# Two weight loads on two DMA queues at once, and the activations behind the first of them

## The chip, the cores and the metric

The kernel runs on one core of a Trainium2 chip. The metric is the device time of one execution in microseconds; a comparison is made between medians of runs. A core has five engines that run their own instruction streams and meet at semaphores: TensorE (PE in the profile), VectorE (DVE), ScalarE (ACT), GpSimd (POOL) and SyncE (SP). A transfer between memory and the on-chip buffer is issued by an engine's instruction stream into that engine's DMA queue; here SyncE's queue is q1 and ScalarE's is q10 in the profile's table. The same 16 DMA engines serve both.

## What is computed

One decoding step for a batch of two tokens: attention over a cache of 8192 keys for 32 heads of width 128, multiplied by a gate from a small MLP.

```
xn = layernorm(x)                                  # x: 2 x 512
q  = xn @ wq                                       # 512 x 4096, 32 heads of 128
p  = softmax(q . k_cache * 128**-0.5)              # k_cache: 2 x 32 x 8192 x 128, fp32
s  = (p . v_cache) @ wo                            # v_cache the same size, wo: 4096 x 512
y  = layernorm(xn)
g  = silu(gelu(y @ w1 + b1) @ w2 + b2)             # w1: 512 x 1376, w2: 1376 x 512
out = x + s * g
```

The two caches are 537 MB of the 559 MB that are read.

## The kernel before

The kernel writes out every engine's order by hand. Each operation is put on record with the keys that it reads and writes, and a small planner (`Plan.op`) derives the semaphore waits from these keys; the instructions of each engine are then emitted in the order in which they were recorded. The order of the code is therefore the order on each engine and on each DMA queue.

The caches are worked off in 32 tiles, each of two heads of one token (a "pair" here): a tile of K is 128 partitions by 64 KB, 8.39 MB, and so is a tile of V. There are two K buffers, `kb[0]` and `kb[1]`, and one V buffer, `vb`. For each pair n, VectorE multiplies the K tile by q in place in two halves (L510), sums each product over the head width (L516) and takes the maximum (L520, L525). ScalarE takes the exponentials (L535). TensorE multiplies them with the V tile (L551). K of pair n+2 is issued by SyncE when the sums of pair n are done; V of pair n is issued when L551 of pair n-1 is done. All of these loads pass through the one helper `load` (L315) on SyncE's queue.

Before the first pair there is a start-up in which no V tile is in `vb` yet, and the MLP's weights and rows lie there instead. wq lies in `kb[0]`, the buffer into which K of pair 1 goes. The order of SyncE's queue at the start is w1, w2, wq, K of pair 0 in two halves (into `kb[1]`), then K of pair 1, which waits until the q projection (L480) has read wq, then V of pair 0, which waits for the last reader of the MLP's tiles. ScalarE's queue carries x (4 KB, two rows), b1 and b2.

The compute of the start-up is one chain. x is copied into a second layout (L380, L382); layer norm (L361 to L366) gives xn, a second layer norm gives y; both are transposed on TensorE and copied by ScalarE (L373, L374). Then, on TensorE in this order: the first MLP product with w1 (L408, with b1 at L410), the rearrangement of its result and the GELU, the second product with w2 (L450) and b2 (L460), the q projection (L480), and the spreading of q over all partitions into `Q` (L493, L495). VectorE's first L510 waits for the first part of `Q` and for K of pair 0.

After the last pair, wo is loaded into `vb` in five pieces and the output projection (L621, L630) and the gate close the kernel.

Of the kernel before, what the change touches and what calls it, by code (L numbers as in the profile page):

```python
# [20 lines left out]
class Plan:  # L21
# [18 lines left out]
    def op(self, eng, fn, r=(), w=(), over=(), it=None, dma=None):  # L40

        o = Op()
        o.eng, o.fn, o.it, o.dma, o.tell = eng, fn, it, dma, False
        need = {}

        def after(d, war):
            if d.dma is None and dma is None and d.eng == eng and (eng == "pe" or war):
                return
            if d.dma is None:
                if need.get(d.eng) is None or need[d.eng].idx < d.idx:  # L50
                    need[d.eng] = d
            else:
                k = ("dma", d.dma)
                if need.get(k) is None or need[k].idx < d.idx:
                    need[k] = d

        for k in r:
            if k in self.writer:
                after(self.writer[k], False)
        for k in list(w) + list(over):  # L60
            if k in self.writer:
                after(self.writer[k], False)
            for d in self.readers.get(k, ()):
                after(d, True)
        clock = self.clock[eng]
        need = {k: d for k, d in need.items() if clock.get(k, 0) < d.idx}
        o.deps = [(k, d) for k, d in need.items()
                  if not any(e is not d and e.done.get(k, 0) >= d.idx for e in need.values())]
        for _, d in o.deps:
            for k, v in d.done.items():  # L70
                clock[k] = max(clock.get(k, 0), v)
        own = eng if dma is None else ("dma", dma)
        self.count[own] = o.idx = self.count.get(own, 0) + 1
        o.done = dict(clock)
        o.done[own] = o.idx
        for k in w:
            self.writer[k] = o
            self.readers[k] = []
        for k in r:
            if k not in w:  # L80
                self.readers.setdefault(k, []).append(o)
        self.ops.append(o)
# [87 lines left out]
def decode_kernel(nc, x, kc, vc, wq, wo, w1, b1, w2, b2, out):  # L170
    P = 128
# [27 lines left out]
    plan = Plan(nc)  # L199
    op = plan.op  # L200
# [7 lines left out]
    def act(fn, r=(), w=()):  # L208
        op("act", fn, r, w)
# [53 lines left out]
    def take(name, p, n, base=0, at=None):  # L263

        if at is None:
            at = used[0]
            used[0] += n
            assert used[0] <= KP * DH
        boot.append(name)
        return vb[base:base + p, at:at + n]  # L270

    w1_sb = take("w1", P, ND * F).rearrange("p (c f) -> p c f", f=F)
    w2_sb = take("w2", P, WB * P)
# [3 lines left out]
    x_sb, xn, y = (take(k, B, D, 0, at + D * i) for i, k in enumerate(("x", "xn", "y")))  # L277
# [26 lines left out]
    def bank():  # L304
        i = turn[0] % 4
        turn[0] += 1
        return scratch[i], f"s{i}"
# [3 lines left out]
    vf = vc.rearrange("b h s d -> (b h s d)").rearrange("(n p j d) -> n p j d", p=P, j=KP, d=DH)  # L311
    M = KP // 2

    def load(dst, src, sem, w, over=()):
        op("sp", lambda: nc.sync.dma_start(dst, src), (), w, over=over, dma=sem)  # L315

    def load_k(n, halves=False):
        i = (n + 1) % 2
        if halves:
            for s in range(2):  # L320
                load(kbuf[i][:, s * M:(s + 1) * M], kf[n][:, s * M:(s + 1) * M], f"k{i}{s}", [("kb", i, s)])
        else:
            load(kbuf[i], kf[n], f"k{i}", [("kb", i, s) for s in range(2)])
# [4 lines left out]


    load(w1_sb, w1.rearrange("(p c) f -> p c f", p=P), "w1", ["w1"])  # L330
    load(w2_sb, w2.rearrange("f n -> (f n)").rearrange("(p e) -> p e", p=P), "w2", ["w2"])
    load(wq_sb, wq.rearrange("(p c) n -> p c n", p=P), "wq", [("kb", 0, s) for s in range(2)])
    load_k(0, halves=True)


    dve(lambda: nc.vector.memset(eps_t, EPS), w=["eps"])
    act(lambda: nc.scalar.activation(warm, eps_t, AF.Sqrt), ["eps"], ["warm"])
    op("act", lambda: nc.scalar.dma_start(x_sb, x.rearrange("b s d -> (b s) d")), w=["x"], dma="x")
    for t, src, k in ((b1_sb, b1, "b1"), (b2_sb, b2, "b2")):
        op("act", lambda t=t, src=src: nc.scalar.dma_start(  # L340
            t.rearrange("o (k e) -> o k e", k=16), src.rearrange("(o k e) -> o k e", o=1, k=16)), w=[k], dma=k)
# [144 lines left out]
    for k in range(N // NB):  # L486

        b, e = divmod(k, HH // NB)
        i, g = divmod(e, GQ)
        p, kp = bank()  # L490
# [114 lines left out]
    for b in range(B):  # L605
# [7 lines left out]
                                        op=ALU.mult), ["OA", "rl"], ["on"])  # L613
# [27 lines left out]
    for b in range(B):  # L641
        eng = "sp" if b % 2 == 0 else "act"
# [29 lines left out]
```

## Time and profile before

| what | value |
|---|---|
| time, median of 3 runs | 1300.59 us (1300.42 to 1301.28) |
| profiled execution, its own time | 1301.38 us |
| its span | 1299.3 us |
| DVE busy | 1132.8 us, 87% of the span |
| PE busy | 404.6 us, 31% |
| ACT busy | 77.7 us, 6% |
| DMA | 559.39 MB, mean 431 GB/s |

The span is the stretch between the first and the last instruction that the profiler recorded; the execution's own time has 2.1 us more around it. Shares of busy time are averages over the start-up, 32 pairs and the end. A row of the chain of waits tells what the program was waiting for at each time, followed back from the last instruction; a row of the timeline has the start in us, the duration, the engine, the line, the operation with its tiles, and in brackets how long the engine had been idle and what released it. In the table of DMA issues a landing is the time from the issue to the semaphore that tells that all data are there.

### The profile page before, as it was taken

The numbers are of one execution on the slowest core, as the hardware profiler recorded it, in microseconds if no ns is written. First come the engines' busy times: TensorE is split into PE (matmuls) and PEld (weight loads), VectorE is DVE, ScalarE is ACT, GpSimd is POOL, SyncE is SP. The second block draws the span as 40 slices with busy tenths as digits, with TensorE's granted clock in tenths as the row PEclk, the third lists the DMA queues.
The fourth block names the chain that finished last, engine by engine and source line by source line (L and its number), as shares of the span: only waits on it lengthen the run. The fifth ranks groups of instructions, "written<-read, shape, count | busy, mean of one in ns | idle before, by whom it ended". The sixth has DMA issues, their size and how long they took to land.

```text
span 1299.3 us, 6271 instructions
## 1 busy us (share of the span) xinstructions
PE 404.6 (31%) x2708; PEld 121.7 (9%) x2708; DVE 1132.8 (87%) x273; ACT 77.7 (6%) x250; POOL 1.4 (0%) x8
## 2 busy tenths in 40 slices
PE   5602333312333311333321333321333331233336
PEld 1100001000101000101000101100001100010102
DVE  3599989988889988889988888988888988888990
ACT  1100000000000000000000000000000000000000
POOL 0000000000000000000000000000000000000000
PEclk9856666556666556666655666655666655666658
DMA  9999999999999999999999999999999999999998
GB/s 408 443 422 444 428 438 430 428 444 424 444 428 436 432 428 444 424 444 428 436 432 428 442 426 444 426 438 430 430 440 428 442 428 438 430 430 440 424 434 346
DMA packets 10831, 559.39 MB, mean 431 GB/s; under 512 B 1212, under 2 KB 1220, under 8 KB 1480
## 3 DMA queue, kind: packets, MB, share of 16 engines
q1 hardware_dynamic: 10808, 559.29, 99.6%
q8 instruction: 3, 0.05, 0.0%
q14 instruction: 4, 0.03, 0.0%
q10 hardware_dynamic: 16, 0.01, 0.0%
HBM read 559.30 MB, written 0.00 MB: 430 GB/s over the span
## 4 chain that ended last, share of the span: by engine, by line
DMA 74%; PE 24%; issue 0%; DVE 0%; ACT 0%; SPq 0%
DMA vb<-in_A_v_cache_dram 72%; PE po L551 22%; DMA vb<-in_A_wo_dram 2%; PE s L408 1%; DMA vb<-in_B_w_dram 1%; PE po L480 1%; PE s L450 0%; PE wide L621 0%; PE s L410 0%; DVE vb L416 0%; PE acc L630 0%; ACT L429 0%; PE s L457 0%; DVE vb L442 0%; PE s L422 0%
## 5 line engine op out<-in xcount | busy, mean ns | idle before, releaser
L510 DVE TENSOR_TENSOR kb<-kb,Q 128x8192 f32<-128x8192 f32 x64 | 555.5, 8681 | 107.1 <-DMA kb<-in_A_k_cache_dram 98.9
L516 DVE TENSOR_REDUCE sc<-kb 128x64 f32<-128x8192 f32 x64 | 552.3, 8666 | 0.0
L551 PE MATMUL po<-vb,PZ 128*8 128x512 f32 x1984 | 282.9, 734 | 301.4 <-DMA vb<-in_A_v_cache_dram 301.4
L530 PE MATMUL s<-nm,srow 1*128 1x2 f32 x64 | 18.6, 358 | 364.7 <-DVE nm L525 364.7
L551 PEld LDWEIGHTS po<-vb,PZ 128*8 128x8 f32 x1984 | 56.6, 103 | 501.6 <-issue 501.6
L522 PE MATMUL s<-ident,mx 128*1 128x128 f32 x32 | 11.9, 372 | 182.0 <-DVE mx L520 182.0
L556 ACT COPY o<-po 128x512 f32<-128x512 f32 x32 | 18.7, 585 | 546.8 <-PE po L551 546.8
L530 PEld LDWEIGHTS s<-nm,srow 1*128 1x128 f32 x64 | 15.9, 306 | 374.1 <-DVE nm L525 374.1
L531 ACT COPY bias<-s 128x2 f32<-128x2 f32 x32 | 5.1, 160 | 612.1 <-PE s L530 612.1
L558 PE MATMUL s<-mod,o 128*128 128x2 f32 x256 | 33.7, 254 | 22.8 <-ACT o L556 22.8
L558 PEld LDWEIGHTS s<-mod,o 128*128 128x128 f32 x256 | 31.0, 191 | 52.5 <-ACT o L556 52.5
L535 ACT ACTIVATE PZ<-sc,bias 64x128 f32<-64x128 f32 x64 | 25.5, 399 | 1.8
L522 PEld LDWEIGHTS s<-ident,mx 128*1 128x1 f32 x32 | 2.5, 79 | 185.5 <-DVE mx L520 155.0
L565 DVE TENSOR_TENSOR Z<-blk,s 128x8 f32<-128x8 f32 x32 | 4.9, 152 | 12.8 <-PE s L558 12.8
L416 DVE COPY vb<-vb 2x384 f32<-2x384 f32 x4 | 1.8, 500 | 16.1 <-ACT vb L412 16.1
L408 PE MATMUL s<-vb 128*2 128x512 f32 (+1 forms) x24 | 12.4, 669 | 0.6 <-DMA vb<-in_B_w_dram 0.6
L535 ACT ACTIVATION_READ_ACCUMULATOR PZ<-sc,bias 64x1 f32 x64 | 11.8, 185 | 0.0
L639 DVE TENSOR_TENSOR gate<-acc,gate 128x128 f32<-128x128 f32 x1 | 0.3, 292 | 12.9 <-PE acc L630 12.9
L520 DVE TENSOR_REDUCE mx<-sc 128x1 f32<-128x128 f32 x32 | 9.1, 286 | 1.1
L539 ACT ACTIVATE ZR<-half,rs 128x8 f32<-128x8 f32 x32 | 9.6, 300 | 1.0
L551 PE MATMUL po<-kb,PZ 128*8 128x512 f32 x64 | 9.0, 726 | 1.4 <-ACT PZ L535 1.4
L621 PE MATMUL wide<-vb,on 128*2 128x512 f32 x52 | 7.9, 719 | 3.9 <-DMA vb<-in_A_wo_dram 3.9
(83 smaller groups left out, 79.8 us busy)
## 6 DMA issues: line engine op xcount, KB each, us to landing
kb<-in_A_k_cache_dram SPq DMA_DIRECT2D x4, 4096.0 KB, 43.6
kb<-in_A_v_cache_dram SPq DMA_DIRECT2D x2, 4096.0 KB, 41.2
vb<-in_B_w_dram SPq DMA_DIRECT2D x2, 2752.0 KB, 12.5
vb<-in_A_wo_dram SPq DMA_DIRECT2D x1, 4096.0 KB, 19.5
vb<-in_A_wo_dram SPq DMA_DIRECT2D x1, 2560.0 KB, 25.3
vb<-in_A_wo_dram SPq DMA_DIRECT2D x1, 1024.0 KB, 27.3
vb<-in_A_wo_dram SPq DMA_DIRECT2D x2, 256.0 KB, 27.5
vb<-in_A_v_cache_dram SPq DMA_DIRECT2D x31, 29.5
```

Of the source, the lines that this page charges most:

```text
L408: pe(lambda f=f, w=w, ph=ph, c=c: matmul(ph[:B, :w], yT[:, c, :], w1_sb[:, c, f:f + w], start=(c == 0), stop=False), ["yT", "w1"], [k])
L480: pe(lambda i=i, c=c, wv=wv, a=a, j=j, hd=hd: matmul(PO[R * j:R * j + NQ * B, :].rearrange("m (h d) -> m h d", d=DH), xnT[:, c, a:a + NQ * ...
L510: dve(lambda: nc.vector.tensor_tensor(out=k, in0=k, in1=Q[:, n].unsqueeze(1).to_broadcast([P, M, DH]), op=ALU.mult), [("kb", i, s), ("Q", ...
L516: dve(lambda: nc.vector.tensor_reduce(out=SC[n % 2][:, s * M:(s + 1) * M], in_=k, axis=AX.X, op=ALU.add), [("kb", i, s)], [("sc", n % 2, s)])
L520: dve(lambda: nc.vector.tensor_reduce(out=MX, in_=SC[n % 2], axis=AX.X, op=ALU.max), [("sc", n % 2, 0), ("sc", n % 2, 1)], ["mx"])
L522: pe(lambda: transpose(PM[:1, :P], MX, ident), ["mx", "ident"], ["s1"], it)
L530: pe(lambda: matmul(PN[:, :U], srow, NM, start=True, stop=True), ["srow", "nm"], ["s2"], it)
L535: act(lambda r=r, s=s: nc.scalar.activation(PZ[r, :, s, :], sc[r], AF.Exp, bias=BIAS[r, s:s + 1], scale=SCALE, accum_out=RS[r]), ["bias", ...
L539: act(lambda: nc.scalar.activation(ZR[b][:, UP * hp:UP * (hp + 1)], half, AF.Copy, scale=RS), ["half"] + [("rs", s) for s in range(U)], [( ...
L551: pe(lambda t=t, j=j, v=v: matmul(PO[R * j:R * j + U * JW, :], PZ[:, t].rearrange("p s j -> p (s j)"), v[:, t * JW:(t + 1) * JW, :].rearra ...
L556: act(lambda: nc.scalar.copy(O4, PO), ["po"], ["o4"])
L558: pe(lambda i=i: matmul(PT[:, :U], O4[:, i * DH:(i + 1) * DH], mod[:, i:U * JW:JW], start=(i == 0), stop=(i == JW - 1)), ["o4", "mod"], [" ...
```

## The change

w2's load is issued by ScalarE, as the first instruction of its stream, while SyncE issues w1. x's load moves from ScalarE, where it stood behind the warm-up activation, to SyncE, between w1 and wq. b1 and b2 stay on ScalarE's queue and stand behind w2 there. `load` takes the issuing engine as an argument. No computing instruction is added, removed or reordered; below the edit, all line numbers are one higher.

```diff
-    def load(dst, src, sem, w, over=()):
-        op("sp", lambda: nc.sync.dma_start(dst, src), (), w, over=over, dma=sem)
+    def load(dst, src, sem, w, over=(), eng="sp"):
+        op(eng, lambda: plan.eng[eng].dma_start(dst, src), (), w, over=over, dma=sem)
...
     load(w1_sb, w1.rearrange("(p c) f -> p c f", p=P), "w1", ["w1"])
-    load(w2_sb, w2.rearrange("f n -> (f n)").rearrange("(p e) -> p e", p=P), "w2", ["w2"])
+
+    load(w2_sb, w2.rearrange("f n -> (f n)").rearrange("(p e) -> p e", p=P), "w2", ["w2"], eng="act")
+    load(x_sb, x.rearrange("b s d -> (b s) d"), "x", ["x"])
     load(wq_sb, wq.rearrange("(p c) n -> p c n", p=P), "wq", [("kb", 0, s) for s in range(2)])
     load_k(0, halves=True)
...
     act(lambda: nc.scalar.activation(warm, eps_t, AF.Sqrt), ["eps"], ["warm"])
-    op("act", lambda: nc.scalar.dma_start(x_sb, x.rearrange("b s d -> (b s) d")), w=["x"], dma="x")
```

## The prediction

> **What bounds the kernel now.** I read the strip of forty slices first, then the queue table, then the chain of waits in order of time, and last the timeline and the waits of the first 60 us, where every edited line runs.
>
> From the page, the strips and the queue table:
> ```profile
> DMA  9999999999999999999999999999999999999998
> GB/s 408 443 422 444 428 438 430 428 444 424 444 428 436 432 428 444 424 444 428 436 432 428 442 426 444 426 438 430 430 440 428 442 428 438 430 430 440 424 434 346
> ...
> q1 hardware_dynamic: 10808, 559.29, 99.6%
> ```
> The 16 DMA engines are busy from the first slice to the last but one, on SyncE's queue alone (q1). So 559 MB at 431 GB/s is the time. Work on another engine is free until it makes the queue run dry; then each microsecond of dry queue is a microsecond at the end, because a queue that is always full cannot make up for it.
>
> The chain of waits, in order of time (start us, us, what):
> ```profile
> 0.73 9.48 DMA vb<-in_B_w_dram
> 10.27 6.24 PE s L408 x8
> ...
> 17.45 3.52 PE s L408 x8
> ...
> 38.75 7.02 PE po L480 x64
> 45.79 0.33 SPq L315
> 46.16 48.96 DMA vb<-in_A_v_cache_dram
> 95.12 0.12 issue
> 95.24 9.92 PE po L551 x64
> 105.18 28.65 DMA vb<-in_A_v_cache_dram
> 133.83 0.12 issue
> 133.95 9.34 PE po L551 x64
> 143.31 29.23 DMA vb<-in_A_v_cache_dram
> ```
> w1 opens the MLP at 10.27; the MLP and then the q projection (L480) end at 45.79; only then may K of head pair 1 be issued, into wq's buffer, and V0 behind it. V0 lands at 95.12, V1 at 133.83: 38.71 us for one K and one V tile, so 19.35 us a tile.
>
> The waits of SyncE's own queue say the same from its side:
> ```profile
> SPq L315 <- PE po L480: 42.4, 1, 42.4
> ```
> SyncE has issued w1, w2, wq and K0 in the first 3 us and then stands 42.4 us for L480. These 22.4 MB are the cover for all of the start. Its end: 95.12 less two tiles of 19.35 is 56.4; the longest landing among the first K issues, 53.5 us after an issue at about 2.6, gives 56.1. I take **56.2 for the landing of K0's second half**.
>
> The timeline of the first 12 us (start, us, engine, line, operation), first the x chain:
> ```profile
> 0.89 0.56 ACTq L338 DMA_DIRECT2D vb<-in_A_x_dram  x1
> 4.61 0.60 PE L380 MATMUL s<-vb,ident 2*2 2x128 f32 x8 [4.61 <-DMA vb<-in_A_x_dram]
> 9.66 0.17 ACT L374 COPY vb<-s 128x8 f32<-128x8 f32 x1 [1.44 <-PE s L373]
> 10.27 6.24 PE L408 MATMUL s<-vb 128*2 128x512 f32 x8 [0.64 <-DMA vb<-in_B_w_dram]
> ```
> x lands at 4.61 and is layer-normed twice and transposed by 9.83, which with one handover (0.07) is 9.90: 5.3 us after x. That hides inside w1's own transfer with 0.37 us to spare. The answer for the tile vb in the first 20 us has the landings of w1 and w2:
> ```profile
> DMA to landing us min/median/max: 9.5/12.5/15.6
> ```
> w1 takes 9.5, w2 15.6 from an issue at 1.2, so 16.8 on the clock: 6.6 us for w2's 2.82 MB behind w1. With eight rows on each of 16 DMA engines, a row is 0.82 us. The rest of w1's 9.48, that is 2.9 us, is fixed: issue to first byte, and last byte to release.
>
> **The change, part by part.**
>
> *w2 from SyncE to ScalarE.* SyncE saves an issue (0.4 us), ScalarE gains one ahead of its table load and warm-up activation, which nothing waits for; both 0 on the path. w2 is needed first by L450 at 31.6, 15 us after it lands, so an earlier w2 is worth nothing. Bytes are the same, so w1 and w2 together are done at 16.8 as before, but w1 now shares. If rows alternate, w1's eighth row is the 15th of 16, and w1 lands at 16.0 instead of 10.2. b1 and b2, issued behind w2 on ScalarE's queue, land near 17; L410 wants b1 only after eight L408 matmuls. 0.
>
> *x from ScalarE to SyncE, behind w1.* The costly part. x is two rows of 2 KB on one ring each, where w1's rows stand ahead of it. It lands with or just after w1: between 16.0 and 16.9 by sharing, I take 16.6. Lower bound 10.3, if w1 keeps the whole rate; upper bound 17.7, one more row. So x is 12.0 us later, and its 5.3 us of layer norm and transposes, which used to lie under w1, now stand behind both weights: L408 starts at 16.6 + 5.3 = 21.9 instead of 10.27, **11.6 later**.
>
> *From L408 to the issue of K1.* 45.79 - 10.27 = 35.5 us of PE, ACT and DVE work, unchanged. wq still lands at about 36.2, by its 34.5 us from 1.65, and L480 starts after that in both kernels. One term floats: matmuls after an idle stretch are slow at first. L408's first eight take 6.24 and the next eight 3.52, a surcharge of 2.7; L551's 64, which also start after idleness, take 8.40 to 9.92 in the chain. So a cold start may be up to 1.5 us cheaper or dearer, and L408's is near the dear end. There is a second cold start at L450. I take -0.3, bounds -1.6 and +1.2. **K1 is issued 11.3 later, at 57.1.**
>
> [...]
>
> *What is late next.* K1 cannot land before its issue plus 2.9 plus 19.35: 57.1 + 2.9 = 60.0, where the queue ran dry for landings at 56.2. **Gap: 60.0 - 56.2 = 3.8 us** (bounds with x at 10.3: none, as 51.1 + 2.9 is 54.0; with x at 17.7 and a dear clock: 6.4). It opens once L480 ends more than 7.5 us late.
>
> *Whether a second gap follows.* DVE starts head pair 0 when Q is there, 11.3 later. K2's issue moves from 82.8 to 94.1; with 2.9 it is 97.0, before V0 lands at 95.1 + 3.8 = 98.9: covered by 1.9. The maximum for pair 0 (DVE, 91.57) moves to 102.9, its exponentials follow 2.2 later, so L551 starts at 105.1, no longer when V0 lands, and ends 9.9 later at 115.0. V1 then needs 117.9; K2 keeps the queue until 98.9 + 19.35 = 118.3. Covered by only 0.4. K3 (117.65 becomes 129) is covered by 6. DVE needs 35 us a pair (82.76 to 117.65) against the DMA's 38.7, so it regains 3.7 each time and its 7.5 us of lag behind the DMA are gone after two pairs. No second gap, and nothing of the first is won back, since the DMA then runs full to the end.
>
> **Sum.** The profiled execution took 1301.38 (span 1299.3 and 2.1 around it). Plus 3.8 is 1305.2. The median of the three runs shown is 0.8 lower than that execution, so 1300.6 + 3.8 = **1304.4 us**.
>
> **The rivals.**
>
> *Hidden anyway: 1300.6.* If w1 keeps SyncE's rate until it is done, x lands at 10.3, L408 starts at 15.6, 5.4 late, under the 7.5 of cover. For it: the cover is real, and only 3.8 us are missing. Against: in this run x came through from ScalarE's queue at 4.61 while w1 had rows until 10.2 on the same engines, so the second queue gets its turn after a row or two. A middle way, x at 15.5 with a cheap clock, gives a gap of about 1.5 and 1302. [...]
>
> *A second gap: 1307.* L551 of pair 0 no longer waits for V0 but for DVE, and V1's issue has 0.4 us of cover. A slower start of that L551, or a K1 gap that closes sooner than 2.9 after its issue, opens it; with x at 17.7 and a dear clock the first gap is 6.4 by itself. Against: 9.9 is already the longest L551.
>
> *Faster: 1297.* Two queues feeding the engines at once move w1 and w2 at a higher rate, so that everything behind them comes earlier. The stretch 2 to 3 us moved only 66 GB/s, so there is something to fill. To gain 3.6 us, w1 and w2 (5.64 MB, now 13.0 us at 433 GB/s) would have to pass in 9.4, at 600 GB/s; the page's best slice is 444. And with K0 landing at 52.6, x would have to be there by about 9.2 for K1 not to come late (L408 at 14.5, K1 issued at 49.7). Below either point the gap decides.
>
> **How the numbers follow.** The forecast gap (2.7 to 6 us) 0.62; hidden or nearly so 0.26; second gap or a larger first 0.09; faster 0.03. A change under 0.2%, 2.6 us, can't be told from none. Slower: 0.62 + 0.09 = 0.71; same 0.26, faster 0.03. The range runs from the hidden case at the lowest run shown, 1300.4, to 1306.6, a gap of 6; the forecast's own range is 1303.2 to 1306.6.
>
> **What would show it.** The x matmul (L380, now L381) released near 16.6 and not 4.6; the first MLP matmul near 21.9, released by ScalarE's copy and no longer by w1's DMA; SyncE's wait for the q projection near 54 us; a stretch at 56 to 60 us where the DMA moves nearly nothing; V0's landing near 98.9; L551 of pair 0 waiting for the exponentials, not for V0; from pair 3 on the old rhythm of 38.7, all of it 3.8 later. An x before 13 us proves the sharing wrong; a dry stretch with an unchanged end would prove wrong that the steady state wins nothing back.

## The result, and the profile after

The changed kernel takes 1305.22 us (median of 7 runs, 1304.26 to 1306.89), the kernel before 1300.59 (7 runs, 1300.23 to 1301.57). The ratio is 1.0036, with a 95% interval of 1.0026 to 1.0046: 4.6 us slower. The profiled execution of the changed kernel is the fastest of its seven, 1304.26 us with a span of 1302.9; the seven spans reach from 1302.9 to 1305.5. Against the span before (1299.3) its profile therefore has to account for 3.6 us, not for 4.6.

The strip and the queues of the page, after:

```profile
GB/s 411 405 421 419 449 421 447 423 445 425 443 427 439 431 439 431 423 445 421 449 421 447 423 445 425 443 425 441 427 443 427 427 441 425 445 425 445 422 433 344
...
q1 hardware_dynamic: 10668, 556.48, 98.9%
q10 hardware_dynamic: 156, 2.83, 0.5%
```

w2's 2.8 MB have gone to q10. The second slice (32.6 to 65.1 us) moved 405 GB/s where it had moved 443. Over 32.6 us that is 1.24 MB, or 2.9 us at 431 GB/s: most of the loss lies there. From the third slice on both strips swing about the same rate.

The timeline of the changed kernel's start, then its chain of waits up to the loads:

```profile
0.73 0.42 ACTq L315 DMA_DIRECT2D vb<-in_B_w_dram  x1
1.19 0.33 SPq L315 DMA_DIRECT2D vb<-in_A_x_dram  x1
...
16.75 0.60 PE L381 MATMUL s<-vb,ident 2*2 2x128 f32 x8 [16.75 <-DMA vb<-in_A_x_dram]
...
22.11 5.10 PE L409 MATMUL s<-vb 128*2 128x512 f32 x8 [0.35 <-ACT vb L375]
```
```profile
1.19 15.52 DMA vb<-in_A_x_dram
...
22.11 5.10 PE s L409 x8
...
42.30 4.45 PE s L451 x18
...
48.89 7.03 PE po L481 x64
...
58.39 17.30 DVE kb L511 x2
...
138.88 9.95 PE po L552 x64
148.84 26.90 DMA vb<-in_A_v_cache_dram
175.86 8.53 PE po L552 x64
184.41 29.99 DMA vb<-in_A_v_cache_dram
```

The first MLP product is now released by ScalarE's copy of the transposed y, not by w1. The chain then runs through compute up to 138.88, where it had run through the V loads from 46; V2 lands at 175.74 where it had landed at 172.53. From there the chain is the old one, 3.2 us later, and the last V tile that is awaited in `vb` lands 3.4 us later (at 1259.89 against 1256.52). Nothing is won back. The row of that tile in the chain of waits, first of the changed kernel, then of the kernel before:

```profile
1231.02 28.87 DMA vb<-in_A_v_cache_dram
```
```profile
1226.28 30.23 DMA vb<-in_A_v_cache_dram
```

The landings in the issue table of the changed kernel:

```profile
vb<-in_B_w_dram SPq DMA_DIRECT2D x1, 2752.0 KB, 15.8
...
vb<-in_B_w_dram ACTq DMA_DIRECT2D x1, 2752.0 KB, 16.0
```

Both issued at 0.73, w1 lands at 16.5 and w2 at 16.7: they share the engines evenly, and x comes with them. The trace also keeps a record of every row that was moved (queue, start, duration and size). The records don't name the DMA engine, but a row that starts where another ends can be put behind it. Chained so, they show sixteen engines, and each moves one row of w1 and one of w2 in turn, eight times; w1's last rows end at 14.6 to 15.4 us and w2's at 15.5 to 16.2.

The busy time by stretches, changed kernel (stretch; us of it, then PE, PEld, DVE, ACT and POOL busy; clock, DMA share, GB/s):

```profile
50.00:54.00 4.00, 4.00 (x44) 0.99 (x40) 0.15 (x1) 0.00 (x0) 0.00 (x0) 1.00 0.95 406
54.00:56.00 2.00, 1.87 (x20) 0.29 (x12) 0.00 (x0) 0.06 (x1) 0.00 (x0) 1.00 0.08 33
56.00:58.00 2.00, 1.42 (x8) 0.57 (x10) 0.00 (x0) 0.82 (x2) 0.00 (x0) 1.00 1.50 524
```

A row's bytes are counted in the stretch in which the row starts (K1's first sixteen rows of 64 KB in 2 us are the 524 GB/s). The dry stretch is there, at 54 to 56: all but a few of K0's rows are under way or done, TensorE is still at the q projection, and K1 has not been issued. SyncE's wait for that projection says how late (the waits of SyncE's own queue, changed kernel):

```profile
SPq L315 <- PE po L481: 52.7, 1, 52.7
```

It was 42.4 us, so K1 is issued at 55.9 and not at 45.8.

### The profile page after: what moved, and what is told of

It reads as the page before. It is cut to its first block, busy times and chain, and to the rows that moved or that the text cites. A ratio compares the mean times of both kernels' runs of the same rounds, so it can differ in the third digit from the quotient of the medians.

```text
span 1302.9 us, 6271 instructions
## 1 busy us (share of the span) xinstructions
PE 404.1 (31%) x2708; PEld 121.4 (9%) x2708; DVE 1132.6 (87%) x273; ACT 77.7 (6%) x250; POOL 1.4 (0%) x8
## 4 chain that ended last, share of the span: by engine, by line
DMA 68%; PE 24%; DVE 7%; ACT 0%; issue 0%; SPq 0%; DVEq 0%
DMA vb<-in_A_v_cache_dram 65%; PE po L552 21%; DVE kb L511 3%; DVE sc L517 3%; DMA vb<-in_A_wo_dram 2%; DMA vb<-in_A_x_dram 1%; PE s L409 1%; PE wide L622 1%; PE po L481 1%; PE s L451 0%; PE s L411 0%; DVE vb L417 0%; PE acc L631 0%; ACT L430 0%; PE s L458 0%
## 5 line engine op out<-in xcount | busy, mean ns | idle before, releaser
L552 PE MATMUL po<-vb,PZ 128*8 128x512 f32 x1984 | 283.4, 736 | 285.3 <-DMA vb<-in_A_v_cache_dram 282.7
L552 PEld LDWEIGHTS po<-vb,PZ 128*8 128x8 f32 x1984 | 56.5, 103 | 486.1 <-issue 483.4
L417 DVE COPY vb<-vb 2x384 f32<-2x384 f32 x4 | 1.8, 500 | 14.6 <-ACT vb L413 14.6
L409 PE MATMUL s<-vb 128*2 128x512 f32 (+1 forms) x24 | 11.2, 616 | 0.3 <-ACT vb L375 0.3
## 6 DMA issues: line engine op xcount, KB each, us to landing
vb<-in_A_wo_dram SPq DMA_DIRECT2D x1, 2560.0 KB, 25.6
```

The source lines that it names most:

```text
L409: pe(lambda f=f, w=w, ph=ph, c=c: matmul(ph[:B, :w], yT[:, c, :], w1_sb[:, c, f:f + w], start=(c == 0), stop=False), ["yT", "w1"], [k])
L552: pe(lambda t=t, j=j, v=v: matmul(PO[R * j:R * j + U * JW, :], PZ[:, t].rearrange("p s j -> p (s j)"), v[:, t * JW:(t + 1) * JW, :].rearra ...
```

## The experiments

The edits of loads show the order in which the loads stand in that run, with marks against the changed kernel or the kernel before. A load that is shown at its new place is gone from its old one; loads that are not shown are unchanged.

**w2's move alone.** From the changed kernel:

```diff
+    load(x_sb, x.rearrange("b s d -> (b s) d"), "x", ["x"], eng="act")
     load(w2_sb, ..., "w2", ["w2"], eng="act")
-    load(x_sb, x.rearrange("b s d -> (b s) d"), "x", ["x"])
```

> Only w2's move is kept; x is issued by ScalarE ahead of w2. Theory of the late x: x lands near 4.6 as before, w1 shares and lands near 16.0, L408 starts at 16.1 instead of 10.27, 5.8 late; K1 is issued about 51.5, under the 7.5 us of cover, so no gap: within 1 us of before (1300.6). Rival, the two queues at once lower the DMA rate: 3 to 5 us slower than before, with K0 landing late and no dry stretch.

Measured: 1308.83 us, ratio 1.0066 (1.0052 to 1.008). Neither expectation held. x was there at 4.5 as before and w1 at 14.1, sooner than the first theory's 16.0; then this came (timeline of that kernel):

```profile
14.21 6.45 PE L408 MATMUL s<-vb 128*2 128x512 f32 x8 [4.70 <-DMA vb<-in_B_w_dram]
28.42 1.86 PE L410 MATMUL s<-vb,ones 1*2 1x512 f32 x2 [7.77 <-DMA vb<-in_B_b_dram]
```

TensorE waited 7.8 us for b1, a 5 KB load. The row records tell why. Each of the sixteen engines moved four rows of w1, and from then on a row of w2 and a row of w1 in turn. When w1 was through, at 12.1 to 13.0 us, four of w2's eight rows were left. Two of them followed at once. The other two had to take turns with wq, whose rows are 64 KB, 2.4 us each against 0.8 for a row of w2. The four-byte write with which an engine closes a load took a turn of its own. So w2's last rows ended at 20.2 to 21.1 us, its closing writes came at 22.6 to 23.5, and w2 landed at 23.9, 22.6 us after an issue at 1.33. b1's one row ended at 25.6, behind another row of wq, and its closing write came at 28.0, behind one more.

**The same with b1 and b2 ahead of w2** on ScalarE's queue:

```diff
     load(x_sb, ..., "x", ["x"], eng="act")
+    for t, src, k in ((b1_sb, b1, "b1"), (b2_sb, b2, "b2")):
+        op("act", ...)
     load(w2_sb, ..., "w2", ["w2"], eng="act")
```

> As the run with w2 alone moved, but ScalarE issues x, b1, b2 and only then w2. Theory that the queues alternate row by row and that b1, queued behind w2's rows and each of these behind a 64 KB row of wq, made that run wait 7.8 us at L410: b1 is there by 6, w1 lands at 13 to 14, L408 starts then, K1 is issued at 49 to 50, under the cover: 1300 to 1301. w2 itself should land late, near 26 to 30, yet before L450. Rival, w2 on ScalarE's queue costs as such: still 4 us or more slower.

Measured: 1301.07 us, ratio 1.0005 (0.9996 to 1.0014). The first MLP product starts at 14.39, released by w1, L410 follows it at 20.56 without a wait, K1 is issued at 49.8. w2 needed 31.2 us from its issue and was still in time for L450 at 35.6. Fifteen of its sixteen closing writes came by 25.4 us; the last, at 32.7, was that of the engine that had moved b1 and b2 ahead of its rows of w2. So w2 on the second queue costs nothing by itself; what is queued behind it does.

**x's move alone**, w2 on SyncE's queue behind x:

```diff
     load(w1_sb, ..., "w1", ["w1"])
+    load(x_sb, x.rearrange("b s d -> (b s) d"), "x", ["x"])
     load(w2_sb, ..., "w2", ["w2"])
```

> Only x's move is kept; SyncE issues w1, x, w2. Theory of the late x: x lands with w1 at about 10.3, L408 starts at 15.6, 5.3 late; under the cover: within 1 us of before. Rival, any x behind a weight costs its full delay at the end: 5 us slower.

Measured: 1300.31 us, ratio 0.9996 (0.9987 to 1.0005). x came at 10.6, L408 started at 15.98, K1 was issued at 51.05 and landed at 75.7 as before. Some five microseconds of lateness are free.

**x behind both weights, on one queue:**

```diff
     load(w1_sb, ..., "w1", ["w1"])
     load(w2_sb, ..., "w2", ["w2"])
+    load(x_sb, x.rearrange("b s d -> (b s) d"), "x", ["x"])
```

> One queue only: SyncE issues w1, w2, x. Theory of the late x: w1 lands at 10.2 as before, but x at about 16.8, so L409 starts at about 22.1 and the loss is that of the changed kernel, 1304 to 1306, with a dry stretch of 2.5 to 4 us before K1. Rival, two queues lower the rate: no loss or clearly less, under 1302.

Measured: 1304.43 us, ratio 1.003 (1.0017 to 1.0042), with ScalarE's queue carrying no weight at all. The chain of waits of that kernel:

```profile
1.65 15.40 DMA vb<-in_A_x_dram
17.09 0.65 PE s L380 x8
...
22.44 5.11 PE s L408 x8
...
42.65 4.45 PE s L450 x18
```

x at 17.1, L408 at 22.4, K1 issued at 56.3: the changed kernel over again. The loss is made by where x stands, and the second queue matters only because it makes w1 and w2 finish together.

**TensorE kept warm in the changed kernel.** 75 matmuls of the identity into `wide`, whose content is not needed yet, where TensorE waits: 45 before x's first matmul, 4 before the transposes of xn, 6 before those of y, 8 before L423 and 12 before L451:

```diff
+    def keep_warm(n):
+        for _ in range(n):
+            pe(lambda: matmul(wide[:, :P], ident, ident, start=True, stop=True), ["ident"], ["wide"])
+    keep_warm(45)
     px, kx = bank()
...
+    keep_warm(4)
     transposed(xnT[:, :, (NQ - 1) * B:NQ * B], xn, "xnT", "xn")
```

> The changed kernel with 75 idle matmuls of the identity, put where TensorE waits (for x, between the transposes, before L423 and L451), so that the array is warm. Theory that the cold starts decide the size and the spread: L409's first eight near 3.5 and L451 near 2.5, K1 issued at 51 to 53, under the cover: within 1 us of before, and the seven runs' spread of 2.6 us shrinks to that of before (1.3). Rival, cold starts don't matter: 1304 to 1306 as the changed kernel.

Measured: 1302.73 us (11 runs, 1301.18 to 1304.12), ratio 1.001 (1.0001 to 1.0019). Chain of waits:

```profile
21.89 3.59 PE s L416 x8
...
40.58 2.80 PE s L460 x18
...
45.53 7.03 PE po L490 x64
```

L416 is L409 and L460 is L451 here. The first eight took 3.59 in place of 5.10 and the second product 2.80 in place of 4.45, and K1 was issued at 52.57, 3.4 us earlier. More than half of the loss went. It should all have gone: 52.57 + 2.9 is before 56.2. K1 landed 1.6 us late and V2 2.1. The spread didn't shrink either. Two things were now open: the edge of the cover, and the spread.

**The edge: the kernel before, with operations that only take time.** n multiplications of xn by 1.0 between the layer norms, with n = 12, 16, 19 and 23; all loads as before:

```diff
+    for _ in range(n):
+        dve(lambda: nc.vector.tensor_scalar_mul(xn, xn, 1.0), ["xn"], ["xn"])
     dve(lambda: nc.vector.tensor_reduce(out=mod, ...
```

> The kernel before with 12 VectorE operations of 0.55 us in x's chain, of which 0.37 us lies under w1: K1 issued at 45.8 + 6.2 = 52.0 (the cold starts may shift it by 1.5). Theory of a sharp edge at 53.3 (K0 lands at 56.2, less 2.9): no gap, 1300.6. Rival, a soft edge, as the warm kernel's 2 us for an issue at 52.6 suggests: 1301.5 to 1302.5.

> The kernel before with 23 such operations: K1 issued at 45.8 + 12.3 = 58.1 and no other part of the change. Theory that nothing but the lateness of the MLP's start counts: 4.8 to 6.5 us slower than before, 1305.4 to 1307, a little more than the changed kernel. Rival, the order of the loads itself costs: clearly under the changed kernel's 1305.

> The kernel before with 16 VectorE operations in x's chain; by the runs with 12 and 23 (K1 issued at 50.8 and 55.1) K1 is issued at about 52.4 here, the same as in the warm kernel. Hard edge, loss = issue less 52.6: none, 1300.6. Soft edge, a K1 that is issued in the last 4 us of the queue costs even before it is dry: 1 to 2 us, as the warm kernel's 2.05 at 52.57 says. Rival for that run, the idle matmuls themselves cost: none here.

> The same with 19 operations: K1 issued at about 53.6. Hard edge: 1.0 us slower. Soft edge: 2 us or more, near the loss of the runs on both sides (2.05 at 52.57, 2.5 at 55.09).

An operation took some 0.45 us rather than 0.55, and the cold starts differed (the first eight L410 took 5.79, 6.14, 5.39 and 5.37), so that K1 was issued at 50.8, 53.2, 53.4 and 55.1. Measured for n = 12, 16, 19, 23: 1300.58, 1301.67, 1302.75 and 1303.24 us; ratios 1.0 (0.9991 to 1.0009), 1.0007 (0.9998 to 1.0016), 1.0016 (1.0007 to 1.0025), 1.002 (1.0011 to 1.0029). The run with 12 operations so stayed short of the edge that it was to test. In the run with 16 the interval includes no change; its profiled execution, at 1302.40, lost 1.4 us. The run with 23 came out under 1305, as its rival had it, but with K1 issued 3 us earlier than expected; the table below shows that it loses what its lateness costs.

**The warm kernel, made late** by ten of these operations, with 30 idle matmuls in place of 4 before the transposes of xn:

> The warm kernel with ten more VectorE operations of 0.55 us in x's chain (between the two layer norms), the array kept warm meanwhile; K1 issued at 52.6 + 5.5 = 58.1. Theory of the dry queue: each microsecond past the cover is one at the end, 1305.5 to 1307. If cold starts make the spread of the changed kernel (2.6 us over 7 runs), the spread here is that of before, about 1.4; rival, the spread comes from the refilling queue: again 2.5 or more.

Measured: 1305.64 us (5 runs, 1305.52 to 1307.6), ratio 1.0045 (1.0031 to 1.0059). K1 was issued at 57.5. The size is as expected; the spread of 2.1 us lies between the two expectations. In spans it is 2.3 us (1304.0 to 1306.3), against 0.4 (1299.0 to 1299.4) for the kernel before beside it.

All profiles together, in the order of K1's issue. "Late" is against the kernel before (K1 landed at 75.7, V2 at 172.5); each landing is an issue plus its time to landing, or the end of the chain's DMA row:

| kernel | K1 issued | K1 lands late by | V2 lands late by |
|---|---|---|---|
| before | 45.8 | 0 | 0 |
| w2 alone, b1 first | 49.8 | -0.1 | -0.1 |
| 12 operations | 50.8 | -0.1 | -0.2 |
| x alone | 51.1 | 0 | 0 |
| changed, warm | 52.6 | 1.6 | 2.1 |
| 16 operations | 53.2 | 1.5 | 1.4 |
| 19 operations | 53.4 | 1.8 | 1.8 |
| 23 operations | 55.1 | 1.3 | 2.5 |
| changed | 55.9 | 2.5 | 3.2 |
| x behind both | 56.3 | 3.2 | 3.7 |
| warm, late | 57.5 | 4.2 | 5.0 |
| w2 alone | 60.4 | 7.1 | 7.8 |

From 55 on V2 is late by K1's issue less 52.6, to 0.2 us, whatever made it late: x's place, b1, or idle operations. Up to 51.1 nothing is lost. In between stands a step: an issue at 52.6 to 53.4, which on the straight line would cost 0 to 0.8, costs 1.4 to 2.1. The kernels with 16 and 19 operations have no idle matmuls, so these are not the cause of the warm kernel's loss. Each row of the table is one profiled execution. The runs of the kernels from 52.6 on differ among themselves by 1.7 to 3.2 us in span, and with 16 operations four of eleven runs have spans of 1299.3 or 1299.4, that is, no loss. So the step is what three profiles show; what a typical run of these kernels loses there is less sure.

## Why the prediction came out right, point by point

- **The cover and its end** held. K1 lands 21.9 to 22.6 us after its issue once the queue is dry (2.9 + 19.35 was the estimate, 22.25), and lateness beyond that is paid in full. In the changed kernel K1 took 22.3: by the row records an engine began its first row of K1 1.0 to 1.7 us after the issue, the first rows took 2.5 to 3.4 us in place of 2.42, and the landing came 0.5 us after the last row. The runs with 23 operations and with x behind both weights show it with two other causes. Two readings were off. K0's second half was issued at 2.9, not at 2.6, so it landed at 56.4, which changes the gap by 0.2. And the dry stretch was forecast at 56 to 60 but came at 54 to 56: a landing is that of the last engine (in the changed kernel K0's last row ended at 56.4 and K0 landed at 56.9), and the engines end K0's rows one after another, from 54.1 on.
- **x's landing** was forecast at 16.6, from even sharing by rows; it is 16.7. L409 was forecast at 21.9 and starts at 22.1. w1 was forecast at 16.0 and landed at 16.5, because its closing writes, at 15.5 to 16.2, had to let one more row of w2 pass. The rival in which w1 keeps SyncE's rate (x at 10.3) fell with that. So did the faster one: both weights were in at 16.7 where they had been in at 16.8. An engine's turn was one row, 0.82 us for most rows of 22 KB: the row records of the changed kernel alternate on all sixteen engines. x's two rows started at 15.69 and 15.88, on two engines, each behind that engine's rows and closing writes of w1 and w2.
- **b1 at no cost** held in the changed kernel: L411 follows L409 with no wait. The reason given, that b1 lands with w2, holds only while w2 runs level with w1. In the run with w2 alone moved, w2 was issued 0.6 us after w1, fell behind into the rows of wq, and the same b1 cost 8 us.
- **The cold starts** were mis-sized. The term was the author's estimate, -0.3 with bounds of -1.6 and +1.2; these bounds are what the prediction calls a cheap and a dear clock. L409's first eight took 5.10 and not 6.24, L451 4.45 and not 5.03, together -1.7 and just outside the bounds, so K1 was issued at 55.9 and not at 57.1. The column of the granted clock reads 1.00 from 20 to 30 us, where L409's slow matmuls stand (22.1 to 27.2), and doesn't show them; the run with idle matmuls does, with 3.59 in place of 5.10. By the sum's own formula, an issue at 55.9 gives a gap of 55.9 + 2.9 - 56.2 = 2.6; K1 landed 2.5 late.
- **"No second gap"** held for the issues, but 0.7 us more was lost on a path that the prediction doesn't have. K2 was issued at 92.9, 4.7 us before V0 landed at 97.6, and by the row records none of the sixteen engines paused before its first row of K2. Still K2 landed at 117.6, 20.0 after V0 where a tile takes 19.35. One engine alone was late: at 98.8 it moved a 16 KB packet of the instruction queue (q8) for 0.96 us, its next row took 0.48 us longer, and it ended K2 at 117.1, the others by 116.5. The kernel before has such a packet too, at 88.3, and there it moves V0's last row by less than 0.1 us. Its engines end a tile 1.8 us apart (K0: 54.1 to 55.9), so an engine that ends early can, by estimate, lose 1.5 us unseen; after the dry stretch they end only 1.0 us apart (K1: 76.8 to 77.8). The kernels with 23 operations, with x behind both, with the late warm array and with w2 alone show the same step at K2 (1.2, 0.7, 0.8 and 0.8), with such a packet on one engine in the second row of K2. V1, for which the prediction saw only 0.4 of cover, was issued at 112.6 instead of 115.0, partly because L552 of pair 0 took 8.7 and not 9.9 us, and its landing lost nothing.
- **The sum**, 3.8, came this near in part by luck. In the profiled run the gap is 2.5 because K1 was issued earlier than forecast, and 0.7 was added by the instruction packet: 3.2 at V2, 3.4 at the last V tile awaited in `vb`, 3.6 at the span's end. The median of seven is 4.6, because the profiled run is the fastest of them.
- **The spread** is not explained. In spans, the kernel before varies by 0.7 us from run to run or less and x's move alone by 0.4, but the changed kernel by 2.6. I laid it to cold starts; the late warm kernel, whose array was kept busy (its first eight took 3.59 us), still has 2.3. All eight kernels with K1 issued at 52.6 or later have 1.7 us or more, all others 0.7 or less. So it comes with the gap, but what differs from run to run was not seen, since each kernel has one profile.

## What to carry to other kernels

In a kernel that is bound by its transfers, ask of each load at the start not what it costs but how much lateness of the compute behind it the full queue covers; here 5 us were free and 7 were not (K1 issued 5.3 us late cost nothing at V2, 6.8 us late 2.1). In this kernel a tiny load that begins a long chain belonged ahead of the large ones, on one queue as on two: x behind both weights landed 12.5 and 12.1 us later than at 4.6, and V2 3.7 and 3.2 us later. So did a tiny one that ends a wait: b1 behind w2 made TensorE wait 7.8 us. Here, moving a large load to a second queue made the load beside it land 6.3 us later (16.5 against 10.2) and itself 0.1 us sooner (16.7 against 16.8).

## What the runs showed of the hardware

- The two queues were served row by row on each engine, with rows of 22 KB beside rows of 22 KB (changed kernel) and of 64 KB (w2 alone). The four-byte write that closes a load took a turn like a row: in the kernel before, x's two rows ended at 3.33 and 3.37 us and their closing writes came at 4.16 and 4.20, each behind one row of w1. A queue with 22 KB rows (0.8 us) beside one with 64 KB rows (2.4 us) so got about a quarter of the engines' time: w2 took 22.6 and 31.2 us to land, against 15.6 behind w1 on one queue.
- One 16 KB packet of the instruction queue q8 held one DMA engine for 0.96 to 1.09 us (changed kernel at 98.8, kernel before at 88.3), and the next row on it took 0.48 us longer. In the kernel before this moved the end of a tile by less than 0.1 us; after a dry stretch it cost 0.7 us in the changed kernel.
- A transfer that was issued shortly before the queue ran dry lost time although the queue was not yet dry by the 2.9 us count. K1 issued 2.8 to 3.7 us before K0's landing cost 1.4 to 2.1 us at V2 in three runs; issued 5.2 us before and more, it cost none. By the row records, the engines end K0 one after another between 54.0 and 55.9 us. In these three runs six of the sixteen then stood 0.5 to 2.8 us without a row; the last of them got its first row of K1 3.6 to 4.1 us after the issue, and a first row took up to 4.0 us in place of 2.42. V1 lost nothing at its landing with less than 5 us left, in the late warm kernel (4.2 us before K2's landing) and with w2 alone (4.9). In the warm kernel these microseconds show as a thin stretch, not as a dry one (busy time by stretches):

```profile
54.00:56.00 2.00, 2.00 (x12) 0.72 (x10) 0.97 (x1) 1.17 (x2) 0.00 (x0) 1.00 1.31 459
56.00:58.00 2.00, 2.00 (x13) 0.59 (x10) 2.00 (x1) 1.40 (x3) 0.00 (x0) 1.00 0.95 328
58.00:60.00 2.00, 2.00 (x12) 0.56 (x8) 2.00 (x1) 1.45 (x3) 0.00 (x0) 1.00 0.76 328
```

  The mean of these six microseconds is 372 GB/s; in the kernel before it is 508 (541, 492 and 492). A single stretch of 2 us says little, because rows are counted where they start. Why K1's rows reach some engines late while others are still busy was not settled.
